# One block of a mixture MLP on one core: its first sums collected in one PSUM bank, and a later block's input sums issued further apart

## The chip, the cores and the metric

The kernel runs on one core of a Trainium2 chip. The metric is the device time of one execution in microseconds (us), lower is better. Five engines work side by side, each through its own queue of instructions in a fixed order: TensorE (PE: matmuls), VectorE (DVE), ScalarE (ACT), GpSimd (POOL) and SyncE (SP: issues the loads and stores). Engines wait for each other by semaphores that are built into the program.

## The reference

Three stages: a local and a pooled attention over 2 x 8 heads of 576 positions, one MLP with ELU, and a mixture of four MLPs with ReLU. The change touches only the third.

```python
x = attention(q, k, v)                       # [1152, 512]
h = x @ moe_w_in                             # [1152, 2048]
g = where(h > 0, h, exp(min(h, 0)) - 1)
x = g @ moe_w_out                            # [1152, 512]
p = probs / (probs.sum(-1) + 1e-9)           # [1152, 4]
out = 0
for e in range(4):                           # w1: [512, 1024], w2: [1024, 512]
    out += p[:, e:e+1] * (maximum(x @ w1[e], 0) @ w2[e])
```

## The kernel before

Every float32 operand of a matmul is split into a high and a low part, and each product is three matmuls (high by high, low by high, high by low), issued by `mm3` (L237 to L243, matmuls on L240). So a "product" of `quad` below, with two slices of the inner dimension, is six matmuls of 288 columns.

The mixture (the part under `ph2`) is cut into eight blocks n = 0 to 7: expert e, half s of its 1024 hidden columns. Block 0 is the one that the title speaks of; block 2 is the third. A block first makes the hidden values h (128 x 4 tiles, high and low part, for 1152 tokens in four groups t of 288), then `l2e` multiplies them by w2 and adds the result to `oacc`, for nine tiles of 128 tokens (`psZ`, 12 matmuls a tile).

The products x @ w1 use a scheme with seven products in place of eight: tokens are taken in pairs of groups (`pair` 0 and 1), hidden columns in pairs j, and besides the input blocks themselves (`xbo`) and weight blocks (`wa`) there are differences and sums of them (`xto`, `ws`). **Block 0** does this in `quad(0, j, pair)` (L1065), four times, in the order (j 0, pair 0), (j 1, pair 0), (j 0, pair 1), (j 1, pair 1). A quad makes seven products, each in a PSUM bank of its own taken by `bank("psH")` from a ring of eight. With products numbered as they come:

- 1 is copied by ACT into c1 (`cp`, L1040).
- 2 plus c1 is the first result. A result is finished by `final`: DVE adds in place in PSUM (`add`, L1037), ACT writes the ReLU of it as the high part of h (`hi`, L1043), and DVE writes the rest as the low part (`lo`, L1046), one result later (`flush`), after which the bank is free.
- 3 and 4 are added on DVE to give u2 = c1 + product 3 and u3 = u2 + product 4.
- 5, 6 and 7 are added on DVE to u3, u3 and u2 to give the other three results; before the fifth, DVE also adds product 5 into u2.

So a quad before has seven adds and four low parts on DVE, and one copy and four high parts on ACT. c1, u2 and u3 are three slices of one buffer `cA`, used by every quad.

The inputs `xto[1]` of the quads with pair 1 are made while the quads with pair 0 run, in three steps for each of n = 0 to 3: `xd` (a subtraction on DVE, 576 elements wide, in place in the accumulators `acc`, L880), `xth` (the high part, on ACT, L886) and `xtl` (the low part, on POOL, L890). The four `xd` are not independent: each works on what the one ahead of it wrote or read. They are put into the queues by `first_xt` through the list `due`: entries of (time, ..., function), where time is a nominal clock that each step of a generator moves on by its nominal length (0.8 a product here). `step` (L1287) issues all entries whose time has come ahead of the next step. So `due` sets only the order in the queues.

**Block 2** uses `inner` (L1184) for p = 0, 1 and 3: seven small products of three matmuls each that use four sums of the input as well. The sums for p = 3 are made by `fold(3)` (L1145) in ten steps, spread by times in `due` (L1375): two DVE additions 576 wide (L1154), four DVE subtractions 288 wide (L1157), and four steps with a copy on ACT (`cp`) and a subtraction (L1162), the first on DVE, the other three on POOL. The buffer of these sums is `cC`, which `inner(2, 3)` writes its results into. In the same stretch POOL makes the weight sums of block 2 (`S`, L1010, eight instructions) and the low parts of them (`LS`, L1018, two), which `plan` sets. In `inner` a bank is used for several products in a row: `go(pa, 6, ...)` and `go(pa, 3, ...)` write on into the bank that DVE or ACT has just read.

Of the kernel before, what the change touches and what calls it, by code (L numbers as in the profile page):

```python
# [151 lines left out]
def attn_moe_kernel(  # L152
# [21 lines left out]
    HB = S // 2  # L174
# [18 lines left out]
    s8 = Slots(ctx, tc, "s8", 8)  # L193
# [43 lines left out]
    def mm3(ps, wt, xt, first, last, more=False):  # L237

        for n, (a, b) in enumerate(PASSES):
            nc.tensor.matmul(  # L240
                ps, wt[a], xt[b], start=first and n == 0, stop=last and n == 2, skip_group_check=more
            )
# [167 lines left out]
    with ExitStack() as ph1:  # L410
# [12 lines left out]
        psb_ = Slots(ctx, tc, "psb", 8, space=PSUM)  # L423
# [9 lines left out]
        def bank(name, spare=0, uses=1):  # L433


            ps = psb_.tile([P, 512], F32, name=name, uses=uses)
            for _ in range(spare):
                nc.tensor.matmul(ps[:, :256], identb, junk.to_broadcast([P, 256]), start=True, stop=True)
            return ps
# [334 lines left out]
        def parts64(s):  # L774

            wt[s] = ([], [])
            cols = w_in[:, 2 * s * SB:2 * (s + 1) * SB].rearrange("(k p) (j f) -> j p k f", p=P, j=2)
            rows = w_out[s * SB:(s + 1) * SB].rearrange("(j k p) d -> j p k d", p=P, j=2)
            return [(cols[j], (KD, 256), wt[s][0], 2 * NQ) for j in range(2)] + [
                (rows[j], (2, DM), wt[s][1], 2 * KD * NQ) for j in range(2)  # L780
            ]
# [117 lines left out]
        ws = [weights64(parts64(s), cv) for s in range(NSB)]  # L899
# [123 lines left out]
    with ExitStack() as ph2:  # L1023
# [8 lines left out]
        def dest(j, i, t):  # L1032
            g = hs[2 * j + i][:, :, t * HB:(t + 1) * HB]
            return g[:, 0], g[:, 1]

        def add(o, x, y):
            nc.vector.tensor_tensor(out=o, in0=y, in1=x, op=add_)  # L1037

        def cp(o, x):
            nc.scalar.activation(o, x, AF.Copy)  # L1040

        def hi(d, c):
            nc.scalar.activation(d[0], c, AF.Relu)  # L1043

        def lo(d, c):
            nc.vector.scalar_tensor_tensor(  # L1046
                out=d[1], in0=c, scalar=0.0, in1=d[0].bitcast(F32), op0=ALU.max, op1=sub
            )

        def product(ps, w, x, first=True):  # L1050
            for kk in range(2):
                mm3(ps, (w[:, 0, kk], w[:, 1, kk]), (x[:, 0, kk], x[:, 1, kk]), first and kk == 0, kk == 1, not first)
            return ps

        late = []

        def flush(k=0):

            while len(late) > k:
                d, c, ps = late.pop(0)  # L1060
                lo(d, c)
                if ps is not None:
                    psb_.done(ps)

        def quad(n, j, pair):  # L1065

            wa, ws = wm[n][0][j]
            xb_, xt = xbo[pair], xto[pair]
            c1, u2, u3 = (cA[:, i] for i in range(3))
            t = 2 * pair  # L1070

            def prod(w, x):
                b = bank("psH")
                return b, product(b[:, :HB], w, x)

            def final(w, x, y, i, k):
                b, ps = prod(w, x)
                if i and k:
                    add(u2, u2, ps)
                add(ps, y, ps)  # L1080
                d = dest(j, i, t + k)
                hi(d, ps)
                flush()
                late.append((d, ps, b))

            b, ps = prod(wa[:, 0], xb_[:, 0])
            cp(c1, ps)
            psb_.done(b)
            yield 0.8
            final(wa[:, 1], xb_[:, 1], c1, 0, 0)  # L1090
            yield 0.8
            b, ps = prod(ws[:, 1], xt[:, 1])
            add(u2, c1, ps)
            psb_.done(b)
            yield 0.8
            b, ps = prod(ws[:, 2], xt[:, 2])
            add(u3, u2, ps)
            psb_.done(b)
            yield 0.8
            for w, x, y, i, k in (  # L1100
                (ws[:, 0], xt[:, 0], u3, 1, 1), (wa[:, 2], xt[:, 3], u3, 1, 0), (ws[:, 3], xb_[:, 2], u2, 0, 1),
            ):
                final(w, x, y, i, k)
                if k and not i:
                    s8.done(wa)
                    s8.done(ws)
                yield 0.8

        def l2e(n, t):

# [28 lines left out]
        def xin(p, k):  # L1139

            if k < 3:
                return xq[p][:, k, 0], xq[p][:, k, 1]
            return xsrc(p, 0, 1)

        def fold(p):  # L1145

            xq[p] = up.tile([P, 3, 2, HB], F32R, tag=f"xq{p}", name="xq")
            buf = cC if p == 3 else up.tile([P, 4, HB], F32, tag=f"xq{2 * p + 1}", name="fold")
            f = buf.rearrange("p (a k) b -> p a k b", a=2)
            f11, f21, f12, f22 = (f[:, a, k] for a in range(2) for k in range(2))  # L1150
            tt = nc.vector.tensor_tensor
            for pair in range(2):
                x = (xbo, xbo, None, xto)[p][pair][:, p].bitcast(F32)
                tt(out=f[:, pair], in0=x[:, 0], in1=x[:, 1], op=add_)  # L1154
                yield
            for o, a, b in ((f11, f12, f11), (f12, f22, f12), (f22, f22, f11), (f21, f21, f22)):
                tt(out=o, in0=a, in1=b, op=sub)  # L1157
                yield
            for k, t in ((0, f11), (1, f22), (2, f12), (3, f21)):
                h, l = xin(p, k)  # L1160
                cp(h, t)
                (nc.gpsimd if k else nc.vector).tensor_tensor(out=l, in0=t, in1=h.bitcast(F32), op=sub)  # L1162
                yield
# [120 lines left out]
        due = []  # L1284
        clock = [0.0]
# [41 lines left out]
        def first_xt(n, part):  # L1327
            if part == 0:
                xd(1, n)
            else:  # L1330
                xth(1, n)
                xtl(1, n)

        for n in range(4):
            due += [(0.9 * n, False, lambda n=n: first_xt(n, 0)), (0.9 * n + 0.45, False, lambda n=n: first_xt(n, 1))]
        plan(
# [11 lines left out]
        for pair, j, ts in ((0, 0, ()), (0, 1, ()), (1, 0, (0, 1)), (1, 1, ())):  # L1348
            weave(quad(0, j, pair), iter(()), "")
            if pair:  # L1350
                flush()
            weave(tiles(0, ts), iter(()), "")
        for n in range(len(sbs)):
            m = n + 1
            if n:
                if m < len(sbs):
                    plan(
                        (0, m, "T", 0, 1), (0.5, m, "H", 0, 0), (0.6, m, "L", 0, 0), (4.5, m, "H", 0, 1),
                        (4.6, m, "L", 0, 1), (5, m, "T", 3), (11.6, m, "H", 1, 0), (11.7, m, "L", 1, 0),
                        (11.8, m, "H", 3, 0), (11.9, m, "L", 3, 0), (12, m, "H", 1, 1), (12.1, m, "L", 1, 1),  # L1360
                        (12.5, m, "H", 3, 1), (12.6, m, "L", 3, 1), (12.7, m, "S", 0), (12.8, m, "S", 1),
                        (24.5, m, "HS", 0), (24.6, m, "LS", 0), (25.5, m, "HS", 1), (25.6, m, "LS", 1), (27.5, m, "F2"),
                        (33.5, m, "H2", 0), (33.6, m, "L2", 0), (36.2, m, "H2", 1), (36.3, m, "L2", 1), (36.4, m + 1, "F"),
                    )
                weave(last(n, 0), tiles(n - 1, (6, 7, 8) if n > 1 else (7, 8)), "mgmgmgmgmgmg")
                weave(last(n, 1), tiles(n, (0, 1)), "mgmgmgmgmgmg")
            if m == len(sbs):
                weave(tiles(n, range(2, NTT)), iter(()), "")
                break
            if m == 1:  # L1370
                pre = join(plain(1, 0), plain(1, 1), plain(1, 3), ready(1))
                weave(pre, tiles(0, (2, 3, 4, 5, 6)), "mg" * 20)
                continue
            if m == 2:
                due += [(clock[0] + t, False, lambda g=g: next(g)) for g in [fold(3)] for t in (0, 0.8, 1.6, 2.4, 3.2, 4, 5, 5.1, 5.2, 5.3)]  # L1375
                due.sort(key=lambda x: x[0])
                pre = join(inner(2, 0), inner(2, 1), inner(2, 3), ready(2))
                way = "mmmgmmgmggmg" "mmmgmmgmgm" "gmmmgmmgmggm" "mmgmmgmmgmm"
            else:
                pre = join(inner(m, 0), turns(inner(m, 1), inner(m, 3)), ready(m))  # L1380
                way = "mmmgmmgmggmg" "mmmmgmmgmmgmmgmmgmmg" "mmgmmgmmgmgmg"
            weave(pre, tiles(n, (2, 3, 4, 5)), way)
# [32 lines left out]
```

## Time and profile before

| | us |
|---|---|
| median of 3 runs | 656.12 |
| lowest and highest | 655.24, 656.57 |
| the profiled execution | 657.1 |
| its span in the trace | 655.3 |
| TensorE busy | 645.3 (98%) |
| VectorE busy | 458.5 (70%) |
| GpSimd busy | 313.5 (48%) |
| ScalarE busy | 301.1 (46%) |

The span is the time from the first to the last instruction that the profiler recorded; 1.8 us of the execution lie around it. The granted TensorE clock is full throughout the span. In rows of the trace, times are us from the start of the span. A row "280.31 2.95 PE ... x18" means 18 instructions of one kind in a row from 280.31, that take 2.95 in all; in brackets stands how long the engine was idle ahead of them, and what ended this. Block 0 of the mixture runs from 278.7 to 307.8, the products of block 2 from 355.3 on.

### The profile page before, as it was taken

What the parts mean: (1) busy time and instruction counts of PE and PEld (TensorE: products, weight loads), DVE (VectorE), ACT (ScalarE), POOL (GpSimd) and SP (SyncE); (2) the same over time, 40 slices, a digit from 0 to 9 for tenths busy, and PEclk for the clock granted to TensorE, in tenths of its full rate; (3) what the DMA queues carried; (4) which work ended last, traced back from release to release, by engine and by line L of the source; (5) the groups of instructions that cost most, each with busy time, mean ns of one, the idle gap of its engine ahead of it and who ended that gap; (6) DMA issues with size and microseconds to landing.
All of it is one profiled execution on the core that took longest, in us unless ns stands there. A gap on an engine that the chain in (4) does not pass through costs nothing.

```text
span 655.3 us, 12359 instructions
## 1 busy us (share of the span) xinstructions
PE 645.3 (98%) x4804; PEld 593.2 (91%) x4804; DVE 458.5 (70%) x968; ACT 301.1 (46%) x817; POOL 313.5 (48%) x309
## 2 busy tenths in 40 slices
PE   9999999999999999999999999999999999999998
PEld 5789889999999999999998888988988989989887
DVE  5899999766678784797968665666566565666652
ACT  5898687546564556544414324124143243242110
POOL 5532632303133438365747947629448457377000
PEclk9999999999999999999999999999999999999999
DMA  9999720051141300010210210301201101201012
GB/s 254 189 207 222 166 87 11 1 195 66 65 129 65 130 2 1 2 66 0 65 66 2 83 46 2 128 1 62 69 1 65 65 1 65 64 2 65 1 48 97
DMA packets 40880, 46.70 MB, mean 71 GB/s; under 512 B 23030, under 2 KB 23286, under 8 KB 40822
## 3 DMA queue, kind: packets, MB, share of 16 engines
q1 hardware_dynamic: 40822, 45.91, 24.9%
q8 instruction: 38, 0.62, 0.4%
q14 instruction: 20, 0.16, 0.1%
HBM read 43.55 MB, written 2.36 MB: 70 GB/s over the span
## 4 chain that ended last, share of the span: by engine, by line
PE 85%; DVE 6%; DMA 5%; issue 1%; ACT 1%; SPq 1%; DVEq 0%; ACTq 0%
PE psZ L240 30%; PE psH L240 15%; PE psY L240 12%; PE psE L240 7%; PE psA L240 6%; DMA raw<-in_moe_w_in_dram 4%; PE psG L240 3%; PE psF L240 3%; PE psB L240 2%; PE psX L645 1%; PE psC L240 1%; DMA raw<-in_moe_w_out_dram 1%; PE psP L629 1%; ACT eg L704 1%; DVE w L308 1%
## 5 line engine op out<-in xcount | busy, mean ns | idle before, releaser
L240 PE MATMUL psZ<-wr,h 128*128 128x512 f32 (+2 forms) x876 | 226.8, 391 | 0.0
L240 PEld LDWEIGHTS psZ<-wr,h 128*128 128x128 f32 x876 | 154.5, 188 | 22.0
L240 PE MATMUL psH<-x,w 128*128 128x288 f32 x768 | 108.0, 296 | 1.7 <-DVE w L308 1.4
L240 PE MATMUL psY<-g,w 128*128 128x288 f32 x768 | 106.3, 296 | 0.1
L240 PEld LDWEIGHTS psH<-x,w 128*128 128x128 f32 x768 | 103.3, 188 | 3.2 <-DVE w L308 2.1
L240 PEld LDWEIGHTS psY<-g,w 128*128 128x128 f32 x768 | 103.4, 189 | 0.6 <-DVE g L826 0.3
L1129 DVE SCALAR_TENSOR_TENSOR oacc<-psZ,pn,oacc 128x512 f32<-128x512 f32 (+1 forms) x64 | 47.4, 740 | 45.0 <-PE psZ L240 45.0
L1043 ACT ACTIVATE h<-psF 128x288 fp32r<-128x288 f32 x28 | 11.5, 411 | 119.9 <-DVE psF L1037 119.9
L826 POOL TENSOR_TENSOR g<-gf,g 128x288 fp32r<-128x288 f32 x25 | 22.0, 882 | 80.7 <-ACT g L821 78.1
L1000 POOL TENSOR_TENSOR wq<-raw,wq 128x512 fp32r<-128x512 f32 x21 | 27.0, 1299 | 54.2 <-ACT wq L996 54.2
L240 PEld LDWEIGHTS psE<-xt,ws 128*128 128x128 f32 x336 | 48.6, 188 | 3.3
L240 PE MATMUL psE<-xt,ws 128*128 128x288 f32 x336 | 50.6, 295 | 0.0
L1037 DVE TENSOR_TENSOR c<-psE,c 128x288 f32<-128x288 f32 x56 | 25.5, 457 | 34.6 <-PE psE L240 34.2
L400 POOL TENSOR_TENSOR wr<-raw,wr 128x1024 fp32r<-128x1024 f32 x16 | 38.4, 2405 | 21.5 <-ACT wr L395 19.4
L1010 POOL TENSOR_TENSOR raw<-raw 128x256 f32<-128x256 f32 x56 | 42.6, 765 | 3.4
L821 ACT ACTIVATE g<-gf 128x288 fp32r<-128x288 f32 x64 | 27.4, 441 | 28.3 <-DVE gf L814 21.4
L814 DVE SCALAR_TENSOR_TENSOR gf<-m,psH 128x288 f32<-128x288 f32 x64 | 28.1, 447 | 16.8 <-ACT m L809 12.1
L1037 DVE TENSOR_TENSOR c<-psA,c 128x288 f32<-128x288 f32 x62 | 26.6, 455 | 18.3 <-PE psA L240 18.3
L395 ACT ACTIVATE wr<-raw 128x1024 fp32r<-128x1024 f32 x16 | 16.8, 1058 | 43.4 <-DMA raw<-in_moe_w_dram 23.4
L805 ACT ACTIVATE m<-psH 128x288 f32<-128x288 f32 x64 | 25.5, 407 | 19.6 <-PE psH L240 15.1
L1018 POOL TENSOR_TENSOR ws<-raw,ws 128x1024 fp32r<-128x1024 f32 x14 | 33.9, 2443 | 1.0 <-ACT ws L1014 1.0
L308 POOL TENSOR_TENSOR w<-raw,w 128x512 fp32r<-128x512 f32 x12 | 18.5, 1546 | 30.2 <-ACT w L303 23.2
(169 smaller groups left out, 1215.7 us busy)
## 6 DMA issues: line engine op xcount, KB each, us to landing
raw<-in_moe_w_dram SPq DMA_DIRECT2D x16, 1024.0 KB, 5.1
raw<-in_moe_w_in_dram SPq DMA_DIRECT2D x8, 1024.0 KB, 7.0
raw<-in_moe_w_out_dram SPq DMA_DIRECT2D x8, 1024.0 KB, 5.8
vb<-in_v_dram SPq DMA_DIRECT2D x16, 160.0 KB, 7.9
vraw<-in_v_dram SPq DMA_DIRECT2D x4, 576.0 KB
out_dram<-oacc SPq DMA_DIRECT2D x8, 256.0 KB, 2.0
raw<-in_k_dram SPq DMA_DIRECT2D x2, 576.0 KB, 7.6
raw<-in_q_dram SPq DMA_DIRECT2D x2, 576.0 KB
```

The costliest lines, as they stand in the source:

```text
L240: nc.tensor.matmul(ps, wt[a], xt[b], start=first and n == 0, stop=last and n == 2, skip_group_check=more)
L308: ENG[eng].tensor_tensor(out=t[:, 1, r], in0=up.bitcast(F32), in1=t[:, 0, r].bitcast(F32), op=ALU.subtract)
L400: nc.gpsimd.tensor_tensor(out=t[:, 1], in0=raw[0][:, 2 * j:2 * j + 2], in1=t[:, 0].bitcast(F32), op=ALU.subtract)
L805: nc.scalar.activation(m, ps1["h", s, t, f][:, :HB], AF.Relu, scale=-1.0)
L814: nc.vector.scalar_tensor_tensor(out=gf, in0=m, scalar=-1.0, in1=ps[:, :HB], op0=ALU.add, op1=ALU.max)
L821: nc.scalar.activation(g[:, 0], ps1["gf", s, t, f], AF.Copy)
L826: ENG[eng].tensor_tensor(out=g[:, 1], in0=gf, in1=g[:, 0].bitcast(F32), op=ALU.subtract)
L1000: tt(out=lo, in0=x, in1=hi.bitcast(F32), op=sub)
L1010: tt(out=o, in0=a, in1=b, op=op)
L1018: tt(out=w[:, 1], in0=raw[0][:, :, 2 * j * P:2 * (j + 1) * P], in1=w[:, 0].bitcast(F32), op=sub)
L1037: nc.vector.tensor_tensor(out=o, in0=y, in1=x, op=add_)
L1129: nc.vector.scalar_tensor_tensor(out=a, in0=ps, scalar=sc, in1=a, op0=ALU.mult, op1=ALU.add)
```

## The change

In `quad` the order of the products is another, and three of the seven share a bank: the first product's bank `pa` is kept, a second and a third product are added onto it by TensorE, and ACT copies it out after each (c1, u2, u3). u2 gets one addition from DVE, of the product in bank e. The high part of a result is no longer issued with its addition but two results later (`waits` and `drain`), the low part one later than that. For a quad this makes five adds and four low parts on DVE, three copies and four high parts on ACT, and five banks. The four `xd` of `first_xt` all come ahead of the first quad; `xth` and `xtl` follow from 3 on, 0.8 apart. The ten steps of `fold(3)` get times further apart.

```diff
@@ -1062,6 +1062,16 @@
                 if ps is not None:
                     psb_.done(ps)
 
+        waits = []
+
+        def drain(k=0):
+
+            while len(waits) > k:
+                d, ps, b = waits.pop(0)
+                hi(d, ps)
+                flush()
+                late.append((d, ps, b))
+
         def quad(n, j, pair):
 
             wa, ws = wm[n][0][j]
@@ -1073,38 +1083,37 @@
                 b = bank("psH")
                 return b, product(b[:, :HB], w, x)
 
-            def final(w, x, y, i, k):
-                b, ps = prod(w, x)
-                if i and k:
-                    add(u2, u2, ps)
+            def final(b, y, i, k):
+                ps = b[:, :HB]
                 add(ps, y, ps)
-                d = dest(j, i, t + k)
-                hi(d, ps)
-                flush()
-                late.append((d, ps, b))
-
-            b, ps = prod(wa[:, 0], xb_[:, 0])
-            cp(c1, ps)
-            psb_.done(b)
+                waits.append((dest(j, i, t + k), ps, b))
+                drain(2)
+
+            a, pa = prod(wa[:, 0], xb_[:, 0])
+            cp(c1, pa)
             yield 0.8
-            final(wa[:, 1], xb_[:, 1], c1, 0, 0)
+            b, ps = prod(wa[:, 1], xb_[:, 1])
+            final(b, c1, 0, 0)
             yield 0.8
-            b, ps = prod(ws[:, 1], xt[:, 1])
-            add(u2, c1, ps)
-            psb_.done(b)
+            e, pe = prod(ws[:, 0], xt[:, 0])
             yield 0.8
-            b, ps = prod(ws[:, 2], xt[:, 2])
-            add(u3, u2, ps)
-            psb_.done(b)
+            product(pa, ws[:, 1], xt[:, 1], False)
+            cp(u2, pa)
+            add(u2, u2, pe)
             yield 0.8
-            for w, x, y, i, k in (
-                (ws[:, 0], xt[:, 0], u3, 1, 1), (wa[:, 2], xt[:, 3], u3, 1, 0), (ws[:, 3], xb_[:, 2], u2, 0, 1),
-            ):
-                final(w, x, y, i, k)
-                if k and not i:
-                    s8.done(wa)
-                    s8.done(ws)
-                yield 0.8
+            b, ps = prod(ws[:, 3], xb_[:, 2])
+            final(b, u2, 0, 1)
+            yield 0.8
+            b, ps = prod(wa[:, 2], xt[:, 3])
+            yield 0.8
+            product(pa, ws[:, 2], xt[:, 2], False)
+            cp(u3, pa)
+            psb_.done(a)
+            s8.done(wa)
+            s8.done(ws)
+            final(b, u3, 1, 0)
+            final(e, u3, 1, 1)
+            yield 0.8
 
         def l2e(n, t):
 
@@ -1332,7 +1341,7 @@
                 xtl(1, n)
 
         for n in range(4):
-            due += [(0.9 * n, False, lambda n=n: first_xt(n, 0)), (0.9 * n + 0.45, False, lambda n=n: first_xt(n, 1))]
+            due += [(0, False, lambda n=n: first_xt(n, 0)), (3 + 0.8 * n, False, lambda n=n: first_xt(n, 1))]
         plan(
             (0, 1, "F"), (9.5, 1, "H", 0, 0), (9.6, 1, "L", 0, 0), (17, 1, "H", 1, 0), (17.1, 1, "L", 1, 0),
             (18, 1, "H", 3, 0), (18.1, 1, "L", 3, 0), (20, 1, "S", 0), (20.1, 1, "S", 1), (28.5, 1, "HS", 0),
@@ -1348,6 +1357,7 @@
         for pair, j, ts in ((0, 0, ()), (0, 1, ()), (1, 0, (0, 1)), (1, 1, ())):
             weave(quad(0, j, pair), iter(()), "")
             if pair:
+                drain()
                 flush()
             weave(tiles(0, ts), iter(()), "")
         for n in range(len(sbs)):
@@ -1372,7 +1382,7 @@
                 weave(pre, tiles(0, (2, 3, 4, 5, 6)), "mg" * 20)
                 continue
             if m == 2:
-                due += [(clock[0] + t, False, lambda g=g: next(g)) for g in [fold(3)] for t in (0, 0.8, 1.6, 2.4, 3.2, 4, 5, 5.1, 5.2, 5.3)]
+                due += [(clock[0] + t, False, lambda g=g: next(g)) for g in [fold(3)] for t in (0, 1.1, 2.2, 3.3, 4.4, 5.5, 6.8, 7.6, 8.4, 9.2)]
                 due.sort(key=lambda x: x[0])
                 pre = join(inner(2, 0), inner(2, 1), inner(2, 3), ready(2))
                 way = "mmmgmmgmggmg" "mmmgmmgmgm" "gmmmgmmgmggm" "mmgmmgmmgmm"
```

ScalarE's queue, from the first copy c1 of block 0 on. `c` are the copies c1, u2 and u3, `h` the high parts, `xt` the high parts of `xto[1]` (`xth`):

```order
-L1040 ACTIVATE c_4400<-psH 128x288
+L1040 ACTIVATE c_4400<-psH 128x288 x2
+L886 ACTIVATE xt<-acc 128x576 x3
+L1040 ACTIVATE c_4400<-psH 128x288
+L1043 ACTIVATE h<-psH 128x288 x2
 L886 ACTIVATE xt<-acc 128x576
+L1040 ACTIVATE c_4400<-psH 128x288
 L1043 ACTIVATE h<-psH 128x288
-L886 ACTIVATE xt<-acc 128x576 x3
```

Before, the second quad's c1 stands behind all four `xt` and four `h`. Now u2, three `xt`, u3, two `h` and the fourth `xt` stand between the first quad's c1 and the second's, and these two `h` belong to the first quad's first two results.

VectorE's queue at the same place, before and then after. `acc<-acc` are the four `xd`, `psH` and `c` the adds, `h` the low parts:

```order
L880 TENSOR_TENSOR acc<-acc 128x576
L1037 TENSOR_TENSOR psH<-psH,c_4400 128x288
L880 TENSOR_TENSOR acc<-acc 128x576
L1037 TENSOR_TENSOR c_4400<-psH,c_4400 128x288
L880 TENSOR_TENSOR acc<-acc 128x576
L1037 TENSOR_TENSOR c_4400<-psH,c_4400 128x288
L880 TENSOR_TENSOR acc<-acc 128x576
L1037 TENSOR_TENSOR c_4400<-psH,c_4400 128x288
L1037 TENSOR_TENSOR psH<-psH,c_4400 128x288
L1046 SCALAR_TENSOR_TENSOR h<-psH,h 128x288
```

```order
L880 TENSOR_TENSOR acc<-acc 128x576 x4
L1037 TENSOR_TENSOR psH<-psH,c_4400 128x288
L1037 TENSOR_TENSOR c_4400<-psH,c_4400 128x288
L1037 TENSOR_TENSOR psH<-psH,c_4400 128x288 x3
L1046 SCALAR_TENSOR_TENSOR h<-psH,h 128x288
```

The adds that stood between the four `xd` now stand behind them: the first result's add, the add into u2, and three more results, then the first low part.

GpSimd's queue in block 2, before and then after. `raw` are the weight sums, `ws` their low parts, `xq` and `xt` the low parts of `fold(3)`, `wr` the next weights:

```order
L1010 TENSOR_TENSOR raw_4890<-raw_4890 128x2x128 x8
L1162 TENSOR_TENSOR xq<-c_4402,xq 128x288 x2
L1162 TENSOR_TENSOR xt<-c_4402,xt 128x288
L1018 TENSOR_TENSOR ws<-raw_4890,ws 128x1024 x2
L400 TENSOR_TENSOR wr<-raw_5297,wr 128x1024 x2
```

```order
L1010 TENSOR_TENSOR raw_4882<-raw_4882 128x2x128 x8
L1018 TENSOR_TENSOR ws<-raw_4882,ws 128x1024
L1171 TENSOR_TENSOR xq<-c_4402,xq 128x288
L1018 TENSOR_TENSOR ws<-raw_4882,ws 128x1024
L1171 TENSOR_TENSOR xq<-c_4402,xq 128x288
L1171 TENSOR_TENSOR xt<-c_4402,xt 128x288
L400 TENSOR_TENSOR wr<-raw_5289,wr 128x1024 x2
```

The three low parts of the fold stood ahead of the weights' low parts; now one stands between these and two behind them.

## Rows read from the trace of the kernel before

**Rows 1.** The page, part 1: busy us, share of the span, instructions of each engine.

```profile
PE 645.3 (98%) x4804; PEld 593.2 (91%) x4804; DVE 458.5 (70%) x968; ACT 301.1 (46%) x817; POOL 313.5 (48%) x309
```

**Rows 2.** TensorE's matmuls in order, block 0: start, us, engine, line, what, [idle before].

```profile
278.71 1.76 PE L240 MATMUL psH<-xbo,wa 128*128 128x288 f32 x12
280.31 2.95 PE L240 MATMUL psH<-xt,ws 128*128 128x288 f32 x18
...
284.69 1.76 PE L240 MATMUL psH<-xbo,wa 128*128 128x288 f32 x12
...
288.65 1.07 PE L240 MATMUL psH<-xt,ws 128*128 128x288 f32 x6 [0.60 <-DVE h L1046]
...
291.15 1.76 PE L240 MATMUL psH<-xbo,wa 128*128 128x288 f32 x12
...
296.75 5.65 PE L240 MATMUL psZ<-wr,h 128*128 128x512 f32 x24
```

**Rows 3.** TensorE's matmuls in order, third block.

```profile
359.01 1.55 PE L240 MATMUL psZ<-wr,h 128*128 128x512 f32 x6
361.67 0.66 PE L240 MATMUL psA<-xbo,wq 128*128 128x288 f32 x3 [1.11 <-DVE c L1037]
362.17 0.86 PE L240 MATMUL psZ<-wr,h 128*128 128x512 f32 x3
...
371.89 0.55 PE L240 MATMUL psA<-xq,wq 128*128 128x288 f32 x3
```

**Rows 4.** VectorE in order, block 0.

```profile
281.90 0.75 DVE L880 TENSOR_TENSOR acc<-acc 128x576 f32<-128x576 f32 x1
...
283.97 1.62 DVE L880 TENSOR_TENSOR acc<-acc 128x576 f32<-128x576 f32 x1
...
285.88 1.62 DVE L880 TENSOR_TENSOR acc<-acc 128x576 f32<-128x576 f32 x1
287.42 0.45 DVE L1037 TENSOR_TENSOR c<-psH,c 128x288 f32<-128x288 f32 x1
```

**Rows 5.** GpSimd in order, block 0, a window cut at 284.

```profile
283.44 1.53 POOL L890 TENSOR_TENSOR xt<-acc,xt 128x576 fp32r<-128x576 f32 x1 [2.45 <-ACT xt L886]
```

**Rows 6.** Instructions of L890 from 270 to 292: shortest, median and longest ns.

```profile
L890 POOL TENSOR_TENSOR xt<-acc,xt x5: 1425/1542/1944, 278.4 to 288.7; 128x576 fp32r<-128x576 f32 x5
```

**Rows 7.** ScalarE in order, block 0.

```profile
277.62 1.26 ACT L886 ACTIVATE xt<-acc 128x576 fp32r<-128x576 f32 x2 [0.65 <-DVE acc L880]
...
282.68 0.69 ACT L886 ACTIVATE xt<-acc 128x576 fp32r<-128x576 f32 x1 [2.18 <-DVE acc L880]
...
289.73 0.41 ACT L1043 ACTIVATE h<-psH 128x288 fp32r<-128x288 f32 x1 [0.32 <-DVE psH L1037]
290.04 0.41 ACT L1040 ACTIVATE c<-psH 128x288 f32<-128x288 f32 x1
```

**Rows 8.** VectorE in order, 307 to 316.

```profile
309.57 1.42 DVE L1154 TENSOR_TENSOR fold<-xbo 128x576 f32<-128x576 f32 x2
311.02 5.12 DVE L1157 TENSOR_TENSOR fold<-fold 128x288 f32<-128x288 f32 x2
```

**Rows 9.** GpSimd in order, 300 to 320.

```profile
310.49 5.33 POOL L1018 TENSOR_TENSOR ws<-raw,ws 128x1024 fp32r<-128x1024 f32 x2 [0.96 <-ACT ws L1014]
```

**Rows 10.** All engines in order, third block.

```profile
355.95 7.83 POOL L1010 TENSOR_TENSOR raw<-raw 128x256 f32<-128x256 f32 x8
...
356.13 2.38 DVE L1154 TENSOR_TENSOR c<-xt 128x576 f32<-128x576 f32 x2
...
359.72 1.53 DVE L1157 TENSOR_TENSOR c<-c 128x288 f32<-128x288 f32 x2
361.17 0.45 DVE L1037 TENSOR_TENSOR c<-psA,c 128x288 f32<-128x288 f32 x1
...
365.29 0.80 POOL L1162 TENSOR_TENSOR xt<-c,xt 128x288 fp32r<-128x288 f32 x1
...
366.05 4.74 POOL L1018 TENSOR_TENSOR ws<-raw,ws 128x1024 fp32r<-128x1024 f32 x2
```

## The prediction, as made before the changed kernel was run

> **What bounds the kernel now.** I read the page's first part, then TensorE's matmuls in order in the two places that the change touches, then the queues that feed them. TensorE is busy for 645.3 of a span of 655.3 us [rows 1]. The change removes no matmul and adds none: the quads of block 0 make 4 x 7 products of six before and after. So it can act only through the time that TensorE waits, at two places.
>
> Block 0. The quads begin at 278.71, 284.69 and 291.15, and the third ends at 296.75 [rows 2]. The third is undisturbed: 5.60, or 0.80 a product. The first takes 5.98, the second 6.46, so 0.38 and 0.86 are lost, 1.24 together. The 0.38 lies in the row of 18 matmuls from 280.31: at 0.133 each it should last 2.40 and a tail of 0.16 (rows that follow each other directly overlap by this: 278.71 + 1.76 is 0.16 past 280.31), and it shows 2.95. It is a wait for a low part of `xto` that DVE finishes late. Most of the 0.86 is the idle 0.60 ahead of 288.65, put down to a low part on DVE: a bank that is not free yet. With the overlap it costs 0.76; the first product behind it runs 0.1 slower.
>
> Block 2, `inner(2, 0)`. Idle 1.11 ahead of 361.67 [rows 3]: the last product writes into the bank that DVE has not yet added up. With the overlap this is 1.27, and the three matmuls behind it take 0.50 (362.17 less 361.67) and not 0.40: 1.37 lost. DVE's add there started at 361.17, behind two L1154 (2.38) and three L1157, two of which took 1.53 [rows 10].
>
> So 1.24 + 1.37 = 2.61 us, 0.4% of the time, is all there is to gain.
>
> **What holds DVE up in both places.** A subtraction on DVE with both inputs in SBUF stands still while a POOL instruction runs, and vice versa. Two L1157 of 288 elements took 5.12 [rows 8] beside two L1018 that took 5.33 [rows 9]; an add of the same width that reads PSUM takes 0.45 in the midst of POOL's work [rows 10]. In block 0 the first `xd` (L880) took 0.75, and two later ones, issued while POOL ran L890, 1.62 each [rows 4]. The Trainium skill ("SBUF — State Buffer", section "Who interferes with whom") has it as a rule that a DVE instruction with two SBUF inputs and a GpSimd instruction that reads SBUF exclude each other, and that the one issued first holds the other off to its end. Rows 8 and 9 agree with it, and it speaks against putting four such instructions ahead of the adds.
>
> **Block 0, part by part.** Removed: per quad two adds of DVE (11 instructions become 9, each 0.37 apart), two banks, and the early use of the late low part (that product, `ws[:, 2]`, comes seventh now and not fourth, at 283.5; its low part is done before DVE goes on to the row at 281.90 [rows 4]). The 0.38 is gone. The bank wait goes too: five banks a quad come round later than seven. Two more copies a quad on ACT cost 0.41 each [rows 7], beside TensorE.
>
> Added: TensorE must wait for ACT's copy c1 before it adds product 4 onto the same bank. In the first quad that is free: product 4 starts at 278.71 + 3 x 0.80 = 281.11, and ACT's c1 there has nothing new ahead of it. In the second quad product 4 would start at 278.71 + 10 x 0.80 = 286.71. There ACT's queue has the first quad's second high part and the fourth `xth` ahead of c1. That high part waits for the second result's add on DVE, which stands behind the first result's add, the add into u2, and all four `xd`. So I follow DVE:
> - `xd` 1 starts at 281.90 as before [rows 4]. Each waits for the end of the one ahead, 0.03 later (309.57 + 1.42 = 310.99, next at 311.02 [rows 8]). So `xd` 2 runs 282.68 to 283.43, and `xd` 3 comes at 283.46.
> - POOL's first L890 comes at 283.44 as before [rows 5], since it follows `xd` 1 and `xth` 1 (282.68, 0.69 [rows 7]), which don't move. Alone it takes 1.43 [rows 6], to 284.87. `xd` 3 waits for that and ends 0.65 later, at 285.52 (before, the one issued at 283.97 ended at 285.59).
> - `xd` 4 comes at 285.55, and POOL's second L890 stands ready: it takes its turn behind `xd` 3, as before, and runs to about 286.8. `xd` 4 ends about 287.42 (before: 287.50), and the next DVE instruction starts 0.08 before that, 287.34.
> - First result's add 287.34, add into u2 at 287.71, ending 288.16; the second result's add reads u2, so it runs 288.19 to 288.64.
> - ACT: second high part 288.67; fourth `xth` 0.31 later (the step from 289.73 to 290.04 [rows 7]) at 288.98; c1 0.57 later (277.62: two in 1.26, one 0.69) at 289.55, to 289.96.
> - Product 4 starts at 289.99, 3.28 late, and 0.1 goes with the restart: **3.38 lost**.
>
> From the first result's add to TensorE's start it is 2.65 in this chain. Nothing else is late: product 7 of quad two ends at 293.3, u3, two high parts and the next c1 follow on ACT at steps of 0.31 from 293.5 on, done by 294.9, and product 4 of quad three starts at 295.7. So block 0 changes by -1.24 + 3.38 = +2.14.
>
> The price depends on what `xd` 3 and 4 meet. If no POOL instruction held them, they would run to 284.99, the first result's add would start at 284.91, product 4 at 287.56: 0.85 + 0.1 lost. That is the lower end for this chain, and still a wait. Upper end: the L890 ahead of `xd` 3 takes 1.94, its longest [rows 6], and not 1.43: 0.5 more, 3.9.
>
> **Block 2.** One L1157, half of 1.53 (spacing 0.72), goes behind the add; the two L1154 and two L1157 stay ahead of it. So the add ends at 361.62 - 0.72 = 360.90 and TensorE still waits, 0.54 + 0.1 in place of 1.37. That would bring 0.73. But the low parts of the fold on POOL now stand behind the weights' low parts: the eight L1010 end at 355.95 + 7.83 = 363.78, then L1018 2.37 (half of 4.74), one L1162 0.80, L1018 2.37, two L1162 1.60 [rows 10]: the last ends at 370.92, where before it ended at 366.09. Its input lies in `cC`, which the result of the fourth product of `inner(2, 3)` overwrites; so that add runs 370.95 to 371.40, and the sixth product, into the same bank, starts at 371.43. Before, it started at 371.89 [rows 3]. So this block gains at most 0.46 less a restart of 0.1, not 1.37; a collision of POOL with the first low part (on DVE) takes up to 0.3 of it. I take **0.3**; the ends are 0.05 and, if the eight L1010 run so much faster that POOL is not last, 1.37.
>
> **Sum.** -1.24 + 3.38 - 0.3 = +1.84. It is made on the profiled span of 655.3 (execution 657.1); the runs' median is 656.12, and I put the same difference on it: 656.1 + 1.8 = **657.9**, slower by 0.28%.
>
> **Rivals.**
> - *DVE first at the port.* `xd` 3 comes at 283.46, L890 at 283.44. If `xd` 3 gets in, it ends at 284.21, L890 then runs to 285.56, `xd` 4 to 286.2, the add starts at 286.12, product 4 at 286.12 + 2.65 = 288.77: 2.06 + 0.1 lost. Sum -1.24 + 2.16 - 0.3 = +0.6: 656.7, no difference. It decides by 0.02 us, and the starts of rows need not be when the port is taken; for my forecast speaks that L890 has the earlier start.
> - *No collision*: 0.95 lost, sum -0.6, 655.5. Against it speak both 1.62 rows.
> - *The change as it is meant* (faster): no wait for c1, the load off DVE pays, -1.24 - 0.3 = -1.5, 654.6; with all of block 2, 653.5. It needs the first result's add to start before 286.71 - 2.65 = 284.06, so all four `xd` within 2.2 us of 281.90; at 0.78 each they take 3.1 alone. The Trainium skill ("Perfetto Trace Analysis", section "Optimizing Scalar/DVE Operations") says that moving work from a saturated DVE to ScalarE may pay; by that the time would be this rival's, and the trace shows no ScalarE shortage, only its order.
> - *Worse*: 0.5 more in the chain, 658.4, and with nothing gained in block 2, 658.7.
>
> **How the numbers follow.** A difference under 0.2% (1.3 us) can't be told from none. Chances: forecast 0.5, DVE first 0.25, no collision 0.1, as meant 0.07, worse 0.08. Slower by over 0.2% (above 657.4): 0.43 of the forecast, 0.07 of worse, 0.03 of DVE first: 0.53. Faster (below 654.8): 0.06 of as meant and 0.03 of no collision: 0.09. The rest, 0.38, is no difference. The range runs from 655.4, under the case without a collision, to 658.7; outside lie as meant, part of no collision and half of worse, some 0.17.
>
> **What would show it.** In the changed trace: no gap in the first quad; one idle gap of about 3 us in the second, ahead of six `psH<-xt,ws`, ended by ACT's copy into `c` (L1040); the third and fourth L880 at about 1.6 to 2 us, the first two at 0.75. In block 2 a gap of about half a us ahead of the last product of `inner(2, 0)`, and a second one in `inner(2, 3)`, ended by DVE's add, which itself waits for POOL's last L1171. The forecast is wrong if the gap in the second quad is under 2.5 (then the port went the other way), and the reading of ACT's order is wrong if there is none.

## The result, and the profile after

The changed kernel takes **659.62 us** (median of 10 runs, 658.1 to 661.68) where the kernel before takes 656.35 on the same chip (10 runs, 655.24 to 659.33): a ratio of 1.0051, 95% interval 1.0038 to 1.0065. It is slower, as forecast, but by 3.3 us and not 1.8, and 659.62 lies above the range's upper end of 658.7. The profiled execution has a span of 659.5 and a time of 661.27; its span is 4.2 longer than before's 655.3.

The page of the changed kernel, part 2: the span in 40 slices of 16.5 us, TensorE's busy share and the clock granted to it, in tenths.

```profile
PE   8999999999999999989999999999999999999998
PEclk9999999999999999979999999999999999999999
```

One slice stands out in both rows (the first and the last of PE's row are the two ends of the span), the 18th, from 280.3 to 296.8 us. That is block 0, where the change is. The kernel before shows 9 in the clock row of every slice.

TensorE's waits in the changed kernel, the two that the change touches: who waits for whom, us in total, times, longest.

```profile
PE psH L240 <- ACT c L1040: 3.2, 1, 3.2
...
PE psA L240 <- DVE c L1037: 0.6, 2, 0.3
```

TensorE's matmuls in order, block 0 of the changed kernel: start, us, engine, line, what, count, idle before. It answers to [rows 2].

```profile
278.40 1.76 PE L240 MATMUL psH<-xbo,wa 128*128 128x288 f32 x12
280.00 1.76 PE L240 MATMUL psH<-xt,ws 128*128 128x288 f32 x12
...
284.00 1.76 PE L240 MATMUL psH<-xbo,wa 128*128 128x288 f32 x12
285.60 0.96 PE L240 MATMUL psH<-xt,ws 128*128 128x288 f32 x6
289.77 1.81 PE L240 MATMUL psH<-xt,ws 128*128 128x288 f32 x6 [3.21 <-ACT c L1040]
291.37 1.64 PE L240 MATMUL psH<-xbo,ws 128*128 128x288 f32 x6
292.81 1.64 PE L240 MATMUL psH<-xt,wa 128*128 128x288 f32 x6
294.25 1.49 PE L240 MATMUL psH<-xt,ws 128*128 128x288 f32 x6
295.58 1.76 PE L240 MATMUL psH<-xbo,wa 128*128 128x288 f32 x12
...
301.18 5.65 PE L240 MATMUL psZ<-wr,h 128*128 128x512 f32 x24
```

The quads begin at 278.40, 284.00 and 295.58, and the third ends at 301.18. The first and the third take 5.60, so both losses of before (0.38 and 0.86) are gone. The second takes 11.58. Product 4 is due at 284.00 + 3 x 0.80 = 286.40 and starts at 289.77, 3.37 late. But that explains only part of the 5.98 lost: the four products behind the gap start 1.60, 1.44, 1.44 and 1.33 apart and not 0.80. From 289.77 to 295.58 it is 5.81 for work that takes 3.20 elsewhere: **2.61 more, behind the gap and not in it.**

The same stretch of the changed kernel cut in five. Columns: from and to, us, busy us (and count) of PE, PEld, DVE, ACT and POOL, granted clock, DMA share, GB/s.

```profile
284.00:286.40 2.40, 2.40 (x20) 2.33 (x18) 2.30 (x2) 0.98 (x2) 2.40 (x2) 1.00 0.00 0
286.40:289.77 3.37, 0.17 (x3) 0.00 (x1) 3.00 (x8) 1.75 (x5) 2.23 (x3) 0.82 0.00 0
289.77:291.37 1.60, 1.60 (x6) 1.60 (x7) 0.80 (x2) 0.24 (x1) 1.13 (x1) 0.50 0.00 0
291.37:295.58 4.21, 4.21 (x20) 4.21 (x19) 1.28 (x3) 1.23 (x3) 1.28 (x1) 0.52 0.00 0
295.58:301.18 5.60, 5.60 (x45) 5.60 (x44) 3.56 (x9) 2.34 (x7) 0.00 (x0) 1.00 0.02 4
```

The granted clock is 1.00 up to the gap, falls inside it (0.82 on the mean), stands at 0.50 and 0.52 behind it, that is at the lower of the two levels (1.2 and not 2.4 GHz), and is 1.00 again in the third quad. TensorE is busy through all of the 5.81 us; it is busy at half the clock. Two of the four products take 1.44, less than twice 0.80; why, the rows do not show.

The sum of the differences in this one execution: the quads start 0.31 earlier, block 0 changes by +5.98 - 1.24 = +4.74, and block 2 by -0.30 (below). Together +4.13, against a span 4.2 longer. Nothing else is needed. Single executions differ by a us ahead of block 0 (the quads begin between 276.5 and 279.1 in the profiles of these kernels), so from here on stretches are compared and not spans.

What kept product 4 waiting: the other engines in the changed kernel, in order of start, with the same columns.

```profile
281.59 5.50 DVE L880 TENSOR_TENSOR acc<-acc 128x576 f32<-128x576 f32 x4
...
283.14 5.21 POOL L890 TENSOR_TENSOR xt<-acc,xt 128x576 fp32r<-128x576 f32 x3 [2.45 <-ACT xt L886]
...
287.02 0.45 DVE L1037 TENSOR_TENSOR psH<-psH,c 128x288 f32<-128x288 f32 x1
...
288.43 0.41 ACT L1043 ACTIVATE h<-psH 128x288 fp32r<-128x288 f32 x1 [0.52 <-DVE psH L1037]
288.74 0.68 ACT L886 ACTIVATE xt<-acc 128x576 fp32r<-128x576 f32 x1
...
289.31 0.40 ACT L1040 ACTIVATE c<-psH 128x288 f32<-128x288 f32 x1
```

The single instructions of L880 and L890 in the same place, shortest, median and longest in ns:

```profile
L880 DVE TENSOR_TENSOR acc<-acc x4: 745/1281/2019, 281.6 to 285.3; 128x576 f32<-128x576 f32 x4
L890 POOL TENSOR_TENSOR xt<-acc,xt x3: 1435/1915/1951, 283.1 to 286.4; 128x576 fp32r<-128x576 f32 x3
```

Read it from the top. VectorE's four subtractions `xd` (L880) take 5.50 us in a row: the first two 0.75 and 0.76, the third and fourth, beside GpSimd's low parts (L890), 2.02 and 1.80, where [rows 4] has one at 0.75. The first low part starts 0.03 ahead of the third `xd` (283.14 and 283.17) and takes 1.44, as when it meets nothing. VectorE reaches the first result's add only at 287.02. ScalarE's second high part (288.43), the fourth `xth` (288.74) and then the copy c1 (289.31, done at 289.71) follow one another, and TensorE goes on at 289.77.

Block 2 of the changed kernel, TensorE in order; the rows answer to [rows 3].

```profile
365.20 0.67 PE L240 MATMUL psA<-xbo,wq 128*128 128x288 f32 x3 [0.22 <-DVE c L1037]
...
375.94 0.66 PE L240 MATMUL psA<-xq,wq 128*128 128x288 f32 x3 [0.33 <-DVE c L1037]
```

In place of one idle 1.11 there are two, 0.22 and 0.33. With the overlap of 0.16 and the restart of 0.1 they cost 0.48 and 0.59, together 1.07 where it was 1.37. The second gap ends with VectorE's add, and this add waited for GpSimd's last low part:

```profile
375.43 0.46 DVE L1037 TENSOR_TENSOR c<-psA,c 128x288 f32<-128x288 f32 x1 [1.37 <-POOL xt L1171]
```

The mean granted clock of whole executions of the changed kernel, in order of time:

| time, us | 658.1 | 658.3 | 659.39 | 659.58 | 659.6 | 659.63 | 659.71 | 660.31 | 661.27 | 661.68 |
|---|---|---|---|---|---|---|---|---|---|---|
| mean clock | 1.0 | 1.0 | 0.997 | 0.997 | 0.997 | 0.995 | 0.997 | 0.997 | 0.995 | 0.995 |

The two with a mean clock of 1.0 are 1.75 and 1.95 above before's median of 656.35; the sum of the prediction was +1.84. The other eight carry what the prediction had no term for. Only the execution of 661.27 has a trace; where the clock fell in the others is not recorded.

### The profile page after: what moved, and what is told of

It reads as the page before. It is cut to its first block, busy times and chain, and to the rows that moved or that the text cites. A ratio compares the mean times of both kernels' runs of the same rounds, so it can differ in the third digit from the quotient of the medians.

```text
span 659.5 us, 12355 instructions
## 1 busy us (share of the span) xinstructions
PE 648.1 (98%) x4804; PEld 595.6 (90%) x4804; DVE 455.4 (69%) x960; ACT 302.9 (46%) x825; POOL 314.4 (48%) x309
## 4 chain that ended last, share of the span: by engine, by line
PE 86%; DVE 7%; ACT 2%; DMA 2%; issue 1%; POOL 1%; SPq 0%; DVEq 0%; ACTq 0%
PE psZ L240 29%; PE psH L240 15%; PE psY L240 13%; PE psE L240 7%; PE psA L240 5%; PE psG L240 3%; PE psF L240 3%; PE psB L240 2%; PE psS L585 1%; DMA raw<-in_k_dram 1%; PE psX L645 1%; PE psP L629 1%; DVE acc L880 1%; PE psC L240 1%; PE psGT L736 1%
```

## The experiments

The theory behind the first four: the gap itself is the one forecast, and the rest is TensorE at the lower clock because it had been idle. Rivals: the spread input sums of the third block cost something that the prediction did not see; or the products behind the gap are slow for another reason, such as memory traffic of the other engines.

**The third block's sums as they were.** The changed kernel with the old times of `fold(3)` (`...` in an edit marks what is left out and stays):

```
-    due += [... for t in (0, 1.1, 2.2, 3.3, 4.4, 5.5, 6.8, 7.6, 8.4, 9.2)]
+    due += [... for t in (0, 0.8, 1.6, 2.4, 3.2, 4, 5, 5.1, 5.2, 5.3)]
```

> The changed kernel with the old ten times of fold(3); block 0 as changed. Theory (all of the loss lies in block 0: a gap of 3.4 us ahead of the second quad's fourth product, then 2.6 us of slow products at a lower granted clock; the spread of the fold gains 0.3): 0.3 us slower than the changed kernel, about 659.9 where the kernel before has 656.35, with one idle gap of 1.1 in block 2 as before. Rival (the spread costs part of the loss, by the longer chain on GpSimd): at least 0.5 us faster than the changed kernel, 659.1 or less.

Measured: 659.51 (8 runs), ratio to before 1.0053, interval 1.0037 to 1.007: the changed kernel's own loss without the spreading. The interval is 2 us wide and would not exclude a cost of half a us; the traces do. The idle 1.11 of block 2 is back, and from the first to the last start of a `psA` product in block 2 it is 18.66 us here as in the kernel before (18.65), and 18.39 in the changed kernel. So the spreading does not cause the loss. Block 0 of this kernel in stretches (columns as above):

```profile
284.48:287.84 3.36, 0.16 (x3) 0.01 (x1) 2.99 (x8) 1.75 (x5) 2.23 (x3) 1.00 0.00 0
287.84:292.65 4.81, 4.81 (x25) 4.81 (x26) 2.08 (x5) 1.47 (x4) 2.42 (x2) 0.65 0.00 0
```

The gap is the same to 0.01 us, but here the clock falls only behind it: the four products take 0.89, 1.34, 1.44 and 1.14, 4.81 together, so 1.61 more than 3.20 and not 2.61. The same gap in two kernels gives two different prices, and the price goes with the granted clock (0.65 on the mean here, and 0.50 and 0.52 there).

**The spreading alone.** The kernel before with the new times of `fold(3)`, the same line the other way round.

> The kernel before with the new ten times of fold(3) alone. Theory: two gaps in block 2, 0.4 and 0.5, in place of one of 1.3 and its restart; 0.3 us faster than before, 656.05, within noise. Rival (the spread costs): 0.5 us or more slower, 656.85 or more. Block 0 keeps its gaps of before either way.

Measured: 656.45 (10 runs), ratio 1.0005, interval 0.9994 to 1.0016, so no difference that can be told. Both the forecast gain of 0.3 and the rival's loss of 0.5 are inside the interval, so the time decides nothing. Its trace does show what was forecast: the idle 1.11 becomes 0.21 and 0.32, and block 2 takes 18.39 as in the changed kernel.

**The gap filled with work.** The changed kernel, and in the second quad, just ahead of the waiting product, 28 matmuls of 256 columns into a spare bank that nothing reads. They fill the gap and end at about the time when c1 does:

```
+            if j == 1 and pair == 0:
+                f = bank("psJ", uses=0)
+                for _ in range(28):
+                    nc.tensor.matmul(f[:, :256], identb, junk.to_broadcast([P, 256]), start=True, stop=True)
             product(pa, ws[:, 1], xt[:, 1], False)
```

> The changed kernel with 28 extra matmuls of 256 bf16 columns into a spare bank, ahead of the fourth product of the second quad, about 3.0 us of TensorE work in the gap; the wait for ScalarE's copy stays. Theory (the slow products behind the gap come from the granted clock, which fell because TensorE idled): no slow products, granted clock 1.00 throughout; 656.35 + 1.9 = 658.2, some 1.5 us faster than the changed kernel's 659.6 though TensorE does more. Rival (adding onto a bank that was just read is slow itself, or the clock falls for another reason): products of 1.3 to 1.6 us stay, 659.6 or more.

Measured: 658.0 (10 runs), ratio 1.0021, interval 1.0012 to 1.0031; the mean clock is 1.0 or 0.999 in all ten. On the same chip the kernel without the spreading took 659.51. TensorE in order, then the stretches, of the filled kernel:

```profile
284.01 0.96 PE L240 MATMUL psH<-xt,ws 128*128 128x288 f32 x6
284.81 3.28 PE L1103 MATMUL psJ<-junk,identb 128*128 128x256 bf16 x28
288.18 1.06 PE L240 MATMUL psH<-xt,ws 128*128 128x288 f32 x6
```

```profile
284.81:288.18 3.37, 3.29 (x31) 2.66 (x29) 3.00 (x8) 1.75 (x5) 2.23 (x3) 1.00 0.00 0
288.18:291.47 3.29, 3.29 (x24) 3.29 (x25) 2.07 (x5) 1.48 (x4) 2.02 (x2) 1.00 0.02 5
```

Product 4 is as late as in the changed kernel (288.18 - 284.81 = 3.37), VectorE, ScalarE and GpSimd do the same in the gap, and yet the four products take 3.29, at clock 1.00. Only TensorE's idleness was taken away, and with it went the slow products. The waiting product still adds onto a bank that was just read, and it is not slow. That is the cause shown: **more work on TensorE made the kernel 1.6 us faster** than the changed kernel (658.0 against 659.62; on one chip, 1.5 against the kernel without the spreading, of which 0.3 is the spreading's). What is left, 658.0 - 656.29 = +1.7 against before, is the forecast's +1.84.

The Trainium skill ("TensorE: Matmul & The Clock Gate", section "HAM oscillation — how this bites in real kernels") describes this pattern: TensorE idles while it waits, the clock goes to half, and the work behind the wait starts slow. The rows above agree, with 0.50 and 0.52 behind the gap and 1.00 once it is filled.

**GpSimd's low parts later.** If the 3.37 is made of `xd` waiting for GpSimd, then the gap shrinks when the two no longer meet. The changed kernel with the high and low parts due behind the four subtractions:

```
-    due += [..., (3 + 0.8 * n, False, lambda n=n: first_xt(n, 1))]
+    due += [..., ((4.9, 7.5, 5.7, 6.6)[n], False, lambda n=n: first_xt(n, 1))]
```

> The changed kernel with the four high and low parts of the next pair's inputs (xth, xtl) due at 4.9, 5.7, 6.6 and 7.5, in the order 0, 2, 3, 1, and not from 3 on; the four subtractions on VectorE stay ahead of all. Theory (two of the four subtractions stand still behind GpSimd's low parts, and this makes the gap 3.4 and not about 1): all four subtractions take 0.75 to 0.85 each; the gap shrinks to about 1.1, another of 0.7 may come in the third quad, where a low part is later; no fall of the clock; 656.35 - 1.2 - 0.3 + 2.0 = 656.8, between 656.2 and 657.4. Rival (the gap is made by the place of the copy in ScalarE's queue alone, the collision adds little): the gap stays above 2.5 and the time near 659.

Measured: 657.69 (10 runs), ratio 1.0018, interval 1.0002 to 1.0034, 0.3 above the upper end of what was expected. Its trace, all engines, in order:

```profile
282.24 3.19 DVE L880 TENSOR_TENSOR acc<-acc 128x576 f32<-128x576 f32 x4
...
287.65 0.40 ACT L1040 ACTIVATE c<-psH 128x288 f32<-128x288 f32 x1
...
288.11 1.06 PE L240 MATMUL psH<-xt,ws 128*128 128x288 f32 x6 [0.89 <-ACT c L1040]
```

The four subtractions take 3.19 and not 5.50, and the gap is 0.89 and not 3.21, so the rival (a gap above 2.5) is out. The Trainium skill ("SBUF — State Buffer", section "Who interferes with whom") has the rule that the one of VectorE and GpSimd that issues first holds the other off; the same four instructions at 5.50 and at 3.19 bear it out. A second gap, 0.58, appears in the third quad: ScalarE's high parts there wait for GpSimd's low part, which now comes late, and the copy that ends the gap stands behind them:

```profile
293.48 0.71 ACT L1043 ACTIVATE h<-psH 128x288 fp32r<-128x288 f32 x2 [1.41 <-POOL xt L890]
...
294.55 1.06 PE L240 MATMUL psH<-xt,ws 128*128 128x288 f32 x6 [0.58 <-ACT c L1040]
```

Three of the ten executions have a mean clock of 0.997 (658.22, 658.26 and 660.14), the others 0.999 or 1.0. The median of these seven, 657.25, lies inside what was expected, though at its upper end. So part of the miss goes with the clock; that the clock fell behind these gaps is not shown, as the one trace has it at 1.00, and the rest stays open.

**The results one sum later.** In the changed kernel a result's high part goes to ScalarE once two more results have been added; with three, the second high part no longer stands ahead of c1 in ScalarE's order:

```
-                drain(2)
+                drain(3)
```

> The changed kernel with drain(3) in final: a high part is issued three results later and not two, so one and not two stand ahead of the second quad's copy c1. The collision of VectorE and GpSimd stays. Theory: c1 then waits for the first result's add, one high part and the fourth xth, 0.95 earlier than in the changed kernel; the gap shrinks from 3.4 to about 2.4. If the clock holds, 656.3 - 1.2 + 2.5 = 657.6; if it still falls as in the changed kernel, up to 659.5. Rival (the copy waits for the subtractions on VectorE whatever stands ahead of it): the gap stays at 3.4.

Measured: 658.83 (9 runs), ratio 1.0038, interval 1.0021 to 1.0055. TensorE in order, then the stretch behind the gap, of the profiled execution:

```profile
287.51 1.07 PE L240 MATMUL psH<-xt,ws 128*128 128x288 f32 x6 [2.27 <-ACT c L1040]
288.42 0.96 PE L240 MATMUL psH<-xbo,ws 128*128 128x288 f32 x6
```

```profile
287.51:290.81 3.30, 3.30 (x24) 3.30 (x25) 2.29 (x6) 1.48 (x4) 2.03 (x2) 1.00 0.00 0
```

The gap costs 287.51 - 285.08 = 2.43, as expected and not the rival's 3.4, and the restart 0.10. In this execution (656.54) the clock stays at 1.00, and by the terms it should be -1.24 + 2.43 + 0.10 - 0.30 = +1.0 against before's 655.92; it is +0.6. Seven of the other eight have a mean clock of 0.997 and take 658.31 to 660.35. One, 659.86, is as slow at 1.0, and no profile of it says why. So idling 2.3 us seems to bring the clock down in most executions too; this rests on their mean clocks and times, since none of these eight has a trace. What decides it in a given execution the runs do not show.

**No wait left in block 0.** Both edits together, and the four subtractions `xd` 0.9 apart again, as in the kernel before, so that VectorE reaches the first adds between them:

```
-    due += [(0, False, lambda n=n: first_xt(n, 0)), (3 + 0.8 * n, False, lambda n=n: first_xt(n, 1))]
+    due += [(0.9 * n, False, lambda n=n: first_xt(n, 0)), ((4.9, 7.5, 5.7, 6.6)[n], False, lambda n=n: first_xt(n, 1))]
...
-                drain(2)
+                drain(3)
```

> The changed kernel with three edits of order in block 0: the four subtractions of first_xt 0.9 apart as before; the high and low parts due at 4.9, 5.7, 6.6, 7.5 in the order 0, 2, 3, 1; drain(3). Theory (the new sums cost nothing by themselves, only the order held TensorE up): no gap in block 0, products of 0.80 throughout; 1.2 for block 0 less than before, 0 to 0.3 for the spread: 655.0, between 654.5 and 655.6. Rival (sums in one bank or three copies on ScalarE cost by themselves): gaps of 0.5 or more remain in block 0 and the time is that of before or more.

Measured: 654.19 (5 runs), ratio 0.9968, interval 0.9956 to 0.9981, clock 0.999 or 1.0 in all five. No quad waits any more: they begin at 278.11, 283.70 and 289.30, 5.60 apart. The four `xd` take 0.74 to 0.76 each, and GpSimd's first low part starts at 285.26, behind the last of them (284.15). Against the kernel before that removes 1.24 in block 0 and 0.30 in block 2, 1.54; the medians differ by 655.92 - 654.19 = 1.73. Of the change this keeps the sums in one bank, the later results and the spread sums of block 2. Which of the three edits are needed was not separated.

**And the sums of the third block ahead of the weights.** The prediction found GpSimd's last low part, queued behind the weights' low parts, to be what the second gap of block 2 waits for. So the same kernel with those parts earlier:

```
-    due += [... for t in (0, 1.1, 2.2, 3.3, 4.4, 5.5, 6.8, 7.6, 8.4, 9.2)]
+    due += [... for t in (0, 1.1, 2.2, 3.3, 4.4, 5.5, 5.6, 5.7, 5.8, 5.9)]
```

> As the run without waits in block 0, and fold(3)'s last four steps due at 5.6 to 5.9, so that GpSimd has the three low parts ahead of the weights' low parts again; the first six stay spread. Theory (the second gap of block 2 comes from GpSimd's queue): only the gap of 0.4 ahead of inner(2, 0)'s last product remains in block 2; 0.6 less than the run without waits in block 0: 654.4, between 653.8 and 655.0. Rival (that gap comes back elsewhere): as the run without waits.

Measured: **653.59** (5 runs), ratio 0.9954, interval 0.9941 to 0.9968. It beats both kernels. TensorE in order, the starts of the first three quads and the only wait of block 2 that is left:

```profile
279.06 1.76 PE L240 MATMUL psH<-xbo,wa 128*128 128x288 f32 x12
...
284.66 1.76 PE L240 MATMUL psH<-xbo,wa 128*128 128x288 f32 x12
...
290.26 1.83 PE L240 MATMUL psH<-xbo,wa 128*128 128x288 f32 x12
...
359.95 0.66 PE L240 MATMUL psA<-xbo,wq 128*128 128x288 f32 x3 [0.21 <-DVE c L1037]
```

This execution took 655.38, the slowest of the five, with a mean clock of 0.996. But here the clock is low at the start, as the page's clock row shows:

```profile
PEclk8999999999999999999999999999999999999999
```

It is 0.91 in the first 20 us and 1.00 from there on, through blocks 0 and 2. So a mean clock below 1 does not by itself say that the clock fell behind a gap in block 0; only a trace does.

Of the 2.61 us that the prediction found to be had, all but 0.21 + 0.16 + 0.1 = 0.47 is taken: 2.14, where the medians differ by 2.33.

**The last edit alone.** The kernel before with these times of `fold(3)`:

> The kernel before with fold(3)'s times 0, 1.1, 2.2, 3.3, 4.4, 5.5 and 5.6 to 5.9, nothing else. Theory: of the 1.37 lost in block 2, 0.5 stays and nothing is added; 655.4, 0.9 less than before. Rival: no difference that can be measured, since a wait comes later.

Measured: 655.43 (11 runs), ratio 0.9989, interval 0.998 to 0.9997. Its row in block 2 is also idle 0.21, so 0.90 less than in [rows 3]. The time moved by 0.49, and 0.90 (0.14%) lies within the interval, which just excludes no difference. So the larger part of the 2.33 comes from block 0.

The kernel before with the low parts of block 0 moved as in the fourth experiment was not tried. How much of the gain in block 0 needs the banked products (three of a quad's seven summed in one bank) at all is therefore open.

## Why the prediction was right in its order and wrong in its size

- **What bounds the kernel, and 1.24 gone in block 0**: right. Quads one and three take 5.60.
- **Who waits for what**: right. One gap, in the second quad only, ahead of six `psH<-xt,ws`, ended by ScalarE's copy. VectorE's first add was forecast at 287.34, or 287.03 with the quads' start 0.31 earlier, and came at 287.02; c1 was forecast at 289.55 (289.24) and came at 289.31; product 4 at 289.99 (289.68) and came at 289.77. The third and fourth `xd` were held off as worked out: GpSimd, 0.03 ahead (0.02 was forecast), went first, and the rival "DVE first at the port" did not happen. Gap: forecast 3.28, measured 3.37.
- **Block 2, -0.3**: right by the trace, 1.37 to 1.07, with GpSimd's last low part behind the weights' as what the second gap waits for, in the changed kernel's row at 375.43 and in the experiment that moves it ahead. Too small for the times to show.
- **"0.1 goes with the restart"**: this is the term that failed. It was read from waits of 0.60 and 1.11 idle [rows 2, 3], after which the clock had stayed, and put behind an idle of 3.2, of which the trace of before has none in this part of the kernel. Measured, the restart cost 2.61 in the profiled execution and 1.61 in the kernel without the spreading, because TensorE ran at the lower clock behind the gap; it cost 0.1 where the clock held (behind 2.27 idle in the profile of the kernel with `drain(3)`, and with the gap filled). The sum with 2.6 in place of 0.1 is +4.3 against +4.13 read from the trace.
- **The range**: the text bounded the length of the gap from both sides (0.85 to 3.9) and did not bound the price of restarting at all. Its worst case, 658.7, was a longer gap at full clock. A rival "the clock falls behind the gap" was missing. Priced at half the clock, the four products left in that quad, 3.2 us of work, take up to 3.2 more, so up to 661; that it would be about these four no row of before says.
- **Direction and chances**: slower was given 0.53; it is slower by 0.5%. For the part of +1.84 the reason is the one given; the rest of the 3.3 was not forecast. A time above the range had only half of the 0.08 for "worse", and for another reason than the one that came.

## What to carry to other kernels

A wait on the engine that bounds the kernel has two prices: its length, and what that engine does behind it; where the trace has no gap as long as the one that you forecast, bound the second price from both levels of the clock, not from shorter gaps. An operation moved to an idle engine stands in that engine's order: before moving a copy that the bounding engine will wait for, write down what is ahead of it there and whom that waits for in turn. If such a gap can't be closed, work that nobody needs can be cheaper than idling; but closing it, here by three edits of order together, that keep VectorE's and GpSimd's two-input operations apart and put the results one later, was worth about 5.0 us in one kernel (from 3.3 above the kernel before to 1.7 below it, each on its own chip).

## What the runs showed of the chip that was not expected

- After TensorE idled 3.2 us its clock stood at the lower level in both profiles that have this gap, and the mean clock was below 0.999 in 15 of 18 executions of these two kernels; a kernel with 28 needless matmuls in that place ran faster than without, with no such execution in ten. With 2.27 idle it was seven of nine, with gaps of 0.89 and 0.58 three of ten. In the kernel before, whose gap there is 0.60, it was four of 49 (two of 29 on one chip, two of 20 on the other), so three of ten is too few to tell.
- The same gap did not cost the same twice: 2.61 and 1.61 us in two profiles, and nothing beyond its length in two of ten executions of the changed kernel, by their times. What makes the difference between executions is open.
